# A cosine-attention and GELU kernel: the order of scores, roots and copies in the first batch

## The chip, the cores and the metric

The kernel runs on one core of a Trainium2 chip. The metric is the device time of one execution in microseconds (us). Before the change the median of five runs is 442.06 us (440.85 to 446.4).

## What is computed

For 8 batches, 12 heads, 448 positions and 64 dimensions, the rows of q and k are divided by their norms, scores are divided by tau = 0.1, and softmax and the product with v follow. The heads of a batch are then laid side by side as 3584 rows of 768, which go through two dense layers with an exact GELU between them:

```python
q_n = q / (np.linalg.norm(q, axis=-1, keepdims=True) + 1e-06)
k_n = k / (np.linalg.norm(k, axis=-1, keepdims=True) + 1e-06)
scores = np.matmul(q_n, k_n.transpose(0, 1, 3, 2)) / tau
attn = softmax(scores)            # over the last axis
x = np.matmul(attn, v) -> 3584 x 768
h = x @ w_in                      # 768 x 2048
out = (0.5 * h * (1 + erf(h / sqrt(2)))) @ w_out   # 2048 x 768
```

## The kernel before

The six **pairs** of heads of a batch are numbered g (0 to 5 for the first batch). The 448 positions are four **chunks** of 112. For each pair:

- `load_qk` (L101) brings q and k on SyncE's queue, `load_v` (L115) brings v on GpSimd's queue (its second call serves pairs 1 and 2).
- `square` (L125) and `reduce` (L139) make the sums of squares. Squares of pairs 1 and 2 run on ScalarE, that of pair 3 on VectorE, later ones on GpSimd. All reductions run on VectorE.
- `root` (L151) takes the roots: two small ScalarE operations (`lq`, `root`), then two small VectorE ones (`se`, `rn`).
- `scale` (L170) multiplies q and k by `rn` and writes them as bf16 (`qkb`). GpSimd does it, but for the q half of pair 0, which VectorE does.
- `transposes` (L181) turns `qkb` on TensorE into a PSUM tile `tp`, and VectorE copies it to `qkT`. Pair 0 has two half tiles (`tp0`, `tp0b`) and two half copies (L194); the other pairs of the first batch have one copy (L197). Later batches use a DMA transpose.
- `scores` (L200) multiplies a chunk of k with all of q into the PSUM tile `st`, of which there are two, and ScalarE takes the exponential into `pt` (L209), 192 times in the kernel.
- `columns` (L219) multiplies `pt` of two pairs with ones (`sm`, the sums) or v (`o`). `reciprocals` (L233) and `normalise` (L242) are VectorE's work behind them; `normalise` writes `x`, the input of the dense layers.

The tiles `tp`, `spin`, the second `o` of a pair and later `hp` and `op` share two PSUM banks that `mm_tile` (L89) hands out in turn; `aside=1` asks for the other one without taking a turn.

The order on every engine is the order in which the code is written: scheduling is manual, and each engine runs its list in order, waiting where an operand isn't there. `upto(f, n)` calls f for the next items until n are done. `spin(n)` issues n TensorE matmuls on constants whose result nobody reads. The work before the loop (L461 on) loads, and takes pairs 0 and 1 as far as the scaling. `attention_first` (L327) is the first batch: its loop runs over g, and one turn of it is called a **slot** here. A slot holds the scores of pair g, and beside them the preparation of the pairs behind it and the columns of the pairs ahead of it. Behind the loop the columns of pairs 4 and 5 are done chunk by chunk, and then `first(0)` runs the first dense layer of the batch (`hp`, L432, with the GELU at L454). From the second batch on `attention` interleaves the scores with pieces of the second dense layer (`op`, L268). These parts aren't touched.

Of the kernel before, what the change touches and what calls it, by code (L numbers as in the profile page):

```python
# [15 lines left out]
def kernel(  # L16
# [21 lines left out]
    HP = H // 2  # L38
# [50 lines left out]
    def mm_tile(name, shape=(128, 512), dtype=F32, aside=None):  # L89
        t = ps_mm.tile(list(shape), dtype, tag=f"mm{turn[0] if aside is None else turn[0] ^ aside}", name=name)  # L90
        if aside is None:
            turn[0] ^= 1
        return t
# [19 lines left out]
    NV = len(v_parts)  # L113
# [86 lines left out]
    def scores(g, c0, n=2):  # L200
        qkT = qkT_t[g]
        for c in range(c0, c0 + n):
            st = ps_st.tile([128, 2, 512], F32, tag="st", name=f"st{g}_{c}")
            for h in range(2):
                rows = slice(h * D, (h + 1) * D)
                nc.tensor.matmul(st[:CS, h, :S], lhsT=qkT[rows, 1, c, :], rhs=qkT[rows, 0, :, :],  # L206
                                 start=True, stop=True)
            pt = ptp.tile([CS, 2, S], BF16, tag="pt", name=f"pt{g}_{c}")
            nc.scalar.activation(pt, st[:CS, :, :S], AF.Exp, scale=inv_tau)  # L209
            pt_t[g, c] = pt  # L210
# [8 lines left out]
    def columns(g, n, chunks=range(NC), aside=0):  # L219
        if chunks[0] == 0:  # L220
            bank_t[g, n] = (mm_tile(f"o{g + 1}", aside=aside) if n == 2 else
                            ps_acc.tile([128, 512], F32, tag=("sm", "o")[n], name=("sm", "o")[n] + str(g)))
        for c in chunks:
            for j in range(2):
                for h in range(2):
                    r = 32 * (2 * j + h)
                    w = v_t[g + j][:, h, c, n - 1:D:2] if n else ones
                    nc.tensor.matmul(bank_t[g, n][r:r + 32, :S], lhsT=w, rhs=pt_t[g + j, c][:, h, :],  # L228
                                     start=(c == 0), stop=(c == NC - 1), tile_position=(0, r))
# [3 lines left out]
    def reciprocals(g):  # L233
        tr = rcp.tile([128, S // 32, 32], F32, tag="tr", name=f"tr{g}")
        nc.vector.transpose(tr.rearrange("p b r -> p (b r)"), bank_t.pop((g, 0))[:, :S])  # L235
        rc = rcp.tile([128, S // 32], F32, tag="rc", name=f"rc{g}")
        nc.vector.reciprocal(rc, tr[:, :, 0])
        rs = rcp.tile([128, S // 32, 32], F32, tag="rs", name=f"rs{g}")
        nc.vector.transpose(rs, rc.to_broadcast([128, S // 32, 32]))  # L239
        rs_t[g] = rs.rearrange("p b r -> p (b r)")  # L240

    def normalise(g):  # L242
        b, p = divmod(g, HP)
        rs = rs_t.pop(g)
        for n in (2, 1):
            nc.vector.tensor_tensor(x_t[b][:, p + n - 1, :], bank_t.pop((g, n))[:, :S], rs, ALU.mult)  # L246
# [62 lines left out]
    def upto(f, n, last=NG):  # L309
        while done.get(f, 0) < min(n, last):  # L310
            done[f] = done.get(f, 0) + 1
            f(done[f] - 1)

    def roots(n):
        upto(root, n, len(groups))


    def spin(n):
        if n == 0:
            return  # L320
        ps = mm_tile("spin")
        for _ in range(n):
            nc.tensor.matmul(ps[:CS, :S], lhsT=ident, rhs=blank, start=True, stop=True)  # L323
# [3 lines left out]
    def attention_first():  # L327
        x_t[0] = xp.tile([128, HP, S], BF16, tag="x", name="x0")
        for g in range(HP):
            scores(g, 0)  # L330
            if g == 0:
                upto(square, 4)
                upto(reduce, 4)
                roots(3)
                upto(scale, 3)
                scores(g, 2, 1)
            if g < HP - 1:
                upto(transposes, g + 2)
            upto(reduce, min(g + 4, HP))
            if g == 3:  # L340
                columns(0, 1)
            elif g == 5:
                columns(2, 2, aside=1)
                normalise(2)
            else:
                spin((0, 4, 1, 0, 0)[g])
            if g == 4:
                columns(2, 0)
                reciprocals(2)
            scores(g, *((2, 2) if g else (3, 1)))  # L350
            if g == 2:
                columns(0, 0)
                reciprocals(0)
            if g == 3:
                columns(0, 2, aside=1)
                normalise(0)
            if g == 4:
                columns(2, 1)
            roots(min(g + 4, HP))
            upto(square, (5, 6, 6, 7, 8, 9)[g])  # L360
            upto(scale, min(g + 4, HP))
            upto(reduce, (0, 0, 0, 6, 7, 8)[g])
            upto(load_v, (2, 3, 3, 3, 3, 4)[g], NV)
            upto(load_wi, (1, 2, 3, 4, 4, 4)[g])
            upto(load_qk, (6, 6, 7, 8, 9, 12)[g])
            if g < HP - 2:
                spin((4, 5, 1, 2)[g])
        upto(load_wo, 2)
        upto(reduce, HP + 3)

        for c in range(NC):
            for n in range(3):
                columns(HP - 2, n, (c,))
        reciprocals(HP - 2)
        normalise(HP - 2)

# [95 lines left out]
    upto(square, 3)  # L472
    upto(scale, 1)
    upto(reduce, 2)
    roots(2)
    upto(scale, 2)
    upto(load_v, 2, NV)
    upto(load_wi, 1)
    upto(transposes, 1)
    spin(5)  # L480
    upto(reduce, 3)

    fill = []
    for b in range(B):
        if b == 0:
            attention_first()
        else:
            attention(b, fill)
        first(b)
        sb, hf = divmod(b, 2)  # L490
        todo = [(t, ni) for t in (range(3) if hf == 0 else range(3, 7)) for ni in range(2)]
        if b == 0:
            todo.sort(key=lambda x: x[1])
        fill = [f for t, ni in todo for f in second_pieces(sb, t, ni)]
# [37 lines left out]
```

## Time and profile before

| | |
|---|---|
| median of five runs | 442.06 us |
| the profiled execution, its own time | 442.58 us |
| its span in the trace | 440.5 us |
| first exponential of the first batch starts at | 13.71 us |
| last exponential of the first batch ends at | 38.09 us |
| first dense layer (`hp`) starts at | 39.45 us |
| TensorE busy | 97% of the span |
| ScalarE busy | 60% |
| VectorE busy | 37% |
| GpSimd busy | 46% |

The part that the change rewrites lies between about 9 and 39.45 us of a span of 440.5 us. Times below are microseconds from the start of the span. A busy share says little about one stage; the timeline of a stage, which gives the start, the duration, the line and the tiles of each instruction and what ended the idle time ahead of it, says which engine is waited for. PEclk is the clock that TensorE was granted, as a share of full speed.

### The profile page before, as it was taken

To read this page: it belongs to the slowest core of one execution; us is meant where nothing else is said; L and a number is where in the kernel's file an instruction comes from. 1 tells how busy PE (TensorE), PEld (TensorE's weight loads), DVE (VectorE), ACT (ScalarE), POOL (GpSimd) and SP (SyncE) were. 2 spreads that over 40 slices of the span, in tenths; PEclk is the share of its full clock that TensorE was granted. 3 is DMA by queue.
4 is the path that set the end of the run, shared out by engine and by line. 5 is a ranking of instruction groups with operands and counts; after the bars stand their busy time and mean duration, and the time that the engine had idled before them with its cause. 6 is when DMAs were issued, how large, how long until landed. Compare 5 with 4: busy or idle time off the path is not lost.

```text
span 440.5 us, 7927 instructions
## 1 busy us (share of the span) xinstructions
PE 428.6 (97%) x3294; PEld 216.0 (49%) x3294; DVE 164.8 (37%) x266; ACT 264.0 (60%) x380; POOL 203.3 (46%) x185
## 2 busy tenths in 40 slices
PE   7899999999999999999999999999999999999996
PEld 4444544555444544455444544445444554445563
DVE  4767214650255404542154501753045330341021
ACT  4696577736766467754767449655766458773300
POOL 2799936580834609291571906655190732300000
PEclk9699999999999999999999999999999999999999
DMA  8989999892683918756186743849077500711022
GB/s 228 245 188 209 190 190 214 215 209 63 101 163 83 214 24 112 172 108 159 24 150 146 147 120 45 173 123 207 4 129 152 128 8 1 131 37 36 1 71 71
DMA packets 83635, 54.97 MB, mean 125 GB/s; under 512 B 41872, under 2 KB 78608, under 8 KB 83600
## 3 DMA queue, kind: packets, MB, share of 16 engines
q1 hardware_dynamic: 66416, 42.35, 42.7%
q0 software_dynamic: 16784, 11.80, 18.9%
q8 instruction: 25, 0.41, 0.4%
q10 hardware_dynamic: 400, 0.33, 0.2%
q14 instruction: 10, 0.08, 0.1%
HBM read 45.61 MB, written 11.01 MB: 129 GB/s over the span
## 4 chain that ended last, share of the span: by engine, by line
PE 89%; ACT 5%; DMA 3%; DVE 1%; POOL 1%; SPq 0%; issue 0%; POOLq 0%; ACTq 0%
PE hp L432 33%; PE op L268 31%; PE st L206 10%; PE o L228 8%; PE sm L228 4%; ACT pt L209 4%; DMA qkT<-qkb 2%; DMA qk<-in_k_dram 2%; PE spin L323 1%; PE tp L192 1%; POOL qkb L176 0%; SPq L107 0%; ACT L456 0%; DVE x L246 0%; ACT sq L133 0%
## 5 line engine op out<-in xcount | busy, mean ns | idle before, releaser
L209 ACT ACTIVATE pt<-st 112x896 bf16<-112x896 f32 x192 | 164.7, 915 | 51.7 <-PE st L206 51.2
L268 PE MATMUL op<-wo,g 128*128 128x384 bf16 x896 | 157.9, 327 | 0.0
L432 PE MATMUL hp<-x,wi 128*128 128x448 bf16 x768 | 146.7, 353 | 0.0
L454 ACT ACTIVATE g<-hp 128x448 bf16<-128x448 f32 x128 | 67.1, 545 | 91.7 <-PE hp L432 91.4
L268 PEld LDWEIGHTS <-g 128*128 128x128 bf16 x896 | 81.9, 98 | 70.6 <-issue 21.6
L432 PEld LDWEIGHTS <-wi 128*128 128x128 bf16 x768 | 74.5, 98 | 71.6 <-issue 3.0
L176 POOL TENSOR_TENSOR qkb<-qk,rn 112x512 bf16<-112x512 f32 x95 | 96.8, 1044 | 13.6 <-DVE rn L167 12.2
L137 POOL TENSOR_TENSOR sq<-qk 112x1024 f32<-112x1024 f32 x44 | 82.3, 1888 | 4.4 <-DMA qk<-in_k_dram 4.4
L165 POOL TENSOR_SCALAR se<-sr 112x48 f32<-112x48 f32 x14 | 4.6, 326 | 152.7 <-ACT sr L164 152.6
L149 DVE TENSOR_REDUCE nq<-sq 112x16 f32<-112x1024 f32 x47 | 56.9, 1214 | 36.0 <-POOL sq L137 34.8
L206 PE MATMUL st<-qkT 64*112 64x448 bf16 x384 | 61.4, 380 | 3.4 <-ACT pt L209 3.3
L279 DVE COPY ot<-op 128x384 f32<-128x384 f32 x55 | 29.8, 541 | 78.5 <-PE op L268 78.5
L167 DVE RECIPROCAL rn<-se 112x48 f32<-112x48 f32 (+1 forms) x20 | 7.9, 393 | 103.8 <-POOL se L165 103.5
L228 PE MATMUL o<-pt,v 112*32 112x448 bf16 x768 | 41.4, 353 | 0.2 <-DVE x L246 0.2
L206 PEld LDWEIGHTS <-qkT 64*112 64x112 bf16 x384 | 21.2, 125 | 40.2 <-issue 37.5
L246 DVE TENSOR_TENSOR x<-o,rs 128x448 bf16<-128x448 f32 x48 | 27.8, 620 | 4.3 <-PE o L228 2.0
L235 DVE STREAM_TRANSPOSE tr<-sm 128x448 f32<-128x448 f32 x24 | 15.6, 650 | 35.8 <-PE sm L228 35.8
L228 PEld LDWEIGHTS <-v 112*32 112x32 bf16 x768 | 20.3, 97 | 16.1 <-issue 1.1
L228 PE MATMUL sm<-pt,ones 112*32 112x448 bf16 x384 | 23.1, 355 | 0.0
L323 PE MATMUL spin<-blank,ident 112*112 112x448 bf16 x46 | 13.6, 445 | 4.1 <-DVE qkT L194 2.8
L239 DVE STREAM_TRANSPOSE rs<-rc 128x448 f32<-128x448 f32 x24 | 15.5, 645 | 0.8
L120 POOL DMA_DIRECT2D v<-in_v_dram x17 | 14.0, 823 | 0.0
(37 smaller groups left out, 81.0 us busy)
## 6 DMA issues: line engine op xcount, KB each, us to landing
qk<-in_q_dram SPq DMA_DIRECT2D x48, 224.0 KB, 5.7
qk<-in_k_dram SPq DMA_DIRECT2D x47, 224.0 KB, 6.0
v<-in_v_dram POOLq DMA_DIRECT2D x15, 336.0 KB, 6.2
wi<-in_moe_w_in_dram POOLq DMA_DIRECT2D x4, 768.0 KB, 10.2
wo<-in_moe_w_out_dram POOLq DMA_DIRECT2D x4, 768.0 KB, 19.1
out_dram<-ot SPq DMA_DIRECT2D x7, 336.0 KB, 3.6
out_dram<-ot SPq DMA_DIRECT2D x8, 288.0 KB, 2.6
out_dram<-ot SPq DMA_DIRECT2D x8, 240.0 KB, 3.5
```

Of the source, the lines that this page charges most:

```text
L137: nc.gpsimd.tensor_tensor(sq, t, t, ALU.mult)
L149: nc.vector.tensor_reduce(nq, sq, mybir.AxisListType.X, ALU.add)
L176: eng.tensor_tensor(qkb[:, i].rearrange("p c h d -> p h c d"), t[:, i], rn[:, i].to_broadcast([CS, 2, NC, D]), ALU.mult)
L206: nc.tensor.matmul(st[:CS, h, :S], lhsT=qkT[rows, 1, c, :], rhs=qkT[rows, 0, :, :], start=True, stop=True)
L209: nc.scalar.activation(pt, st[:CS, :, :S], AF.Exp, scale=inv_tau)
L228: nc.tensor.matmul(bank_t[g, n][r:r + 32, :S], lhsT=w, rhs=pt_t[g + j, c][:, h, :], start=(c == 0), stop=(c == NC - 1), tile_position=(0, r))
L246: nc.vector.tensor_tensor(x_t[b][:, p + n - 1, :], bank_t.pop((g, n))[:, :S], rs, ALU.mult)
L268: nc.tensor.matmul(ps[:, :NH], lhsT=g_t[sb][:, kf, t * 128:(t + 1) * 128], rhs=wo[:, kf, ni * NH:(ni + 1) * NH], start=(kf == 0), stop=(kf ...
L279: nc.vector.tensor_copy(ot[:, lo:hi], ps[:, :NH])
L323: nc.tensor.matmul(ps[:CS, :S], lhsT=ident, rhs=blank, start=True, stop=True)
L432: nc.tensor.matmul(hps[m], lhsT=wi[:, kd, m * 128:(m + 1) * 128], rhs=x_t[b][:, kd, :], start=(kd == order[0]), stop=(kd == order[-1]))
L454: nc.scalar.activation(g_t[sb][:, m, hf * S:(hf + 1) * S], hps.pop(m), AF.Gelu)
```

## The change

It alters only the order of the first batch, the number of `spin` matmuls and the bank of one tile.

- Ahead of the loop, the transposes of pair 0 with their two half copies come ahead of `se` and `rn` of pair 1, and two spins follow in place of five. The second load of v leaves this place.
- In slot 0 the chunk-2 scores come ahead of the transposes of pair 1 as before, but the fourth reduction comes behind the copy of pair 1, the roots of pair 2 are the only ones, and the second load of v is issued behind the scaling of pair 2, which is behind the first load of `wi`.
- In slots 1 to 5 the roots of pair g + 2 (in place of g + 3) stand between the first two exponentials and the last two. The transposes of pair g + 1 come behind all four score chunks of pair g. `normalise(0)` comes ahead of the transposes of pair 4.
- Spins per slot were (4), (4, 5), (1, 1), (2) and are (4), (4, 3, 2), (4) and none from slot 3 on.
- Loads of v and `wi` in slots 1 and 2 come ahead of the scaling of pair 4 and of pair 5.
- The second `o` of pairs 2 and 4 swap banks.

```diff
             if g == 0:
                 upto(square, 4)
-                upto(reduce, 4)
                 roots(3)
                 upto(scale, 3)
-                scores(g, 2, 1)
-            if g < HP - 1:
-                upto(transposes, g + 2)
-            upto(reduce, min(g + 4, HP))
-            if g == 3:
-                columns(0, 1)
-            elif g == 5:
-                columns(2, 2, aside=1)
-                normalise(2)
+                upto(load_v, 2, NV)
+                scores(0, 2, 1)
+                upto(transposes, 2)
+                upto(reduce, 4)
+                scores(0, 3, 1)
+                spin(4)
             else:
-                spin((0, 4, 1, 0, 0)[g])
-            if g == 4:
-                columns(2, 0)
-                reciprocals(2)
-            scores(g, *((2, 2) if g else (3, 1)))
-            if g == 2:
-                columns(0, 0)
-                reciprocals(0)
-            if g == 3:
-                columns(0, 2, aside=1)
-                normalise(0)
-            if g == 4:
-                columns(2, 1)
-            roots(min(g + 4, HP))
+                roots(min(g + 3, HP))
+                upto(scale, min(g + 3, HP))
+                if g < 3:
+                    spin(4)
+                elif g == 3:
+                    columns(0, 1)
+                elif g == 4:
+                    columns(2, 0)
+                    reciprocals(2)
+                else:
+                    columns(2, 2)
+                    normalise(2)
+                scores(g, 2)
+                if g == 1:
+                    spin(3)
+                elif g == 3:
+                    columns(0, 2, aside=1)
+                    normalise(0)
+                upto(transposes, min(g + 2, HP))
+                upto(reduce, min(g + 4, HP))
+                if g == 1:
+                    spin(2)
+                elif g == 2:
+                    columns(0, 0)
+                    reciprocals(0)
+                elif g == 4:
+                    columns(2, 1)
             upto(square, (5, 6, 6, 7, 8, 9)[g])
-            upto(scale, min(g + 4, HP))
             upto(reduce, (0, 0, 0, 6, 7, 8)[g])
             upto(load_v, (2, 3, 3, 3, 3, 4)[g], NV)
             upto(load_wi, (1, 2, 3, 4, 4, 4)[g])
             upto(load_qk, (6, 6, 7, 8, 9, 12)[g])
-            if g < HP - 2:
-                spin((4, 5, 1, 2)[g])
...
-                columns(HP - 2, n, (c,))
+                columns(HP - 2, n, (c,), aside=1)
...
     upto(reduce, 2)
+    upto(transposes, 1)
+    spin(2)
     roots(2)
     upto(scale, 2)
-    upto(load_v, 2, NV)
     upto(load_wi, 1)
-    upto(transposes, 1)
-    spin(5)
     upto(reduce, 3)
```

## The prediction

> **What bounds it now.** The page first: TensorE is busy through the span and carries the chain that ended last, and its clock is low in one slice, the second.
>
> ```profile
> PE   7899999999999999999999999999999999999996
>
> PE 89%; ACT 5%; DMA 3%; DVE 1%; POOL 1%; SPq 0%; issue 0%; POOLq 0%; ACTq 0%
> ```
>
> So a stage that starts later on TensorE is not made good behind it, and I take any shift of the first dense layer (`hp`, 39.45) one to one into the end. Second, the stretches of 3.41 us between the clock's steps (us of the stretch, its length, then busy us of TensorE, its weight loads, VectorE, ScalarE, GpSimd, the granted clock, DMA share, GB/s):
>
> ```profile
> 6.49:9.90 3.41, 2.68 (x19) 1.76 (x18) 1.89 (x4) 1.40 (x4) 1.54 (x1) 1.00 1.11 272
> 9.90:13.32 3.42, 1.20 (x7) 0.68 (x8) 2.40 (x6) 1.38 (x3) 1.42 (x2) 1.00 1.18 264
> 13.32:16.73 3.41, 2.77 (x17) 1.34 (x16) 3.34 (x6) 2.94 (x5) 2.10 (x3) 0.50 1.12 258
> 16.73:20.14 3.41, 3.41 (x17) 1.77 (x18) 0.84 (x3) 2.50 (x5) 3.39 (x3) 0.50 1.21 233
> 23.56:26.97 3.41, 2.84 (x34) 1.42 (x32) 2.65 (x5) 3.38 (x6) 3.41 (x4) 1.00 0.59 161
> ```
>
> After a stretch with 1.20 us of 3.42 busy (35%) the clock was 0.50 for 6.82 us; 79% (2.68) and 83% (2.84) kept it, 81% (2.77) at half clock did not bring it back, a full stretch did. Third, the timeline, VectorE and the exponentials:
>
> ```profile
> 9.14 1.22 DVE L149 TENSOR_REDUCE nq<-sq 112x16 f32<-112x1024 f32 x1 [1.13 <-ACT sq L133]
> 11.35 0.19 DVE L160 TENSOR_REDUCE se<-root 112x16 f32<-112x32 f32 x1 [0.99 <-ACT root L159]
> 11.74 0.33 DVE L194 COPY qkT<-tp 128x448 bf16<-128x448 bf16 x1
> 11.98 0.37 DVE L194 COPY qkT<-tp0b 128x448 bf16<-128x448 bf16 x1
> ...
> 30.23 1.16 DVE L246 TENSOR_TENSOR x<-o,rs 128x448 bf16<-128x448 f32 x2 [1.30 <-PE o L228]
> 31.74 0.62 DVE L197 COPY qkT<-tp 128x896 bf16<-128x896 bf16 x1 [0.36 <-PE tp L192]
> ```
>
> ```profile
> 13.71 1.73 ACT L209 ACTIVATE pt<-st 112x896 bf16<-112x896 f32 x2 [2.39 <-PE st L206]
> 18.97 1.73 ACT L209 ACTIVATE pt<-st 112x896 bf16<-112x896 f32 x2 [0.86 <-PE st L206]
> 27.13 1.73 ACT L209 ACTIVATE pt<-st 112x896 bf16<-112x896 f32 x2
> 31.06 1.73 ACT L209 ACTIVATE pt<-st 112x896 bf16<-112x896 f32 x2 [0.32 <-PE st L206]
> ```
>
> The half copies sit 0.99 us behind a root. From 13.71 to the last exponential (38.09), 24 exponentials of 0.87 (half of 1.73) and four roots of 0.5 make 22.9 of 24.4 us: the stage is nearly ScalarE's, and only 2.05 us ahead of it plus 1.5 us of gaps inside are to be had.
>
> **Prices, all from this timeline.** TensorE, full / half clock: the scores of a chunk 0.32 (25.17 to 25.49) / 0.55 (16.09 to 16.64), of two chunks 0.52 / 0.92; from scores' start to exponential 0.44 (30.62 to 31.06) / 0.66 (18.31 to 18.97); transposes 0.50 / 0.86; four spins 0.88 (five took 1.09) / 1.67; `sm` or `o` 0.87. A score tile is free 0.96 behind its exponential's start (13.71 to 14.67). `lq` starts 1.61 behind the first of two exponentials (13.71 to 15.32), the next exponential 0.50 later. GpSimd: scaling 2.04, square 1.88, a DMA issue 0.8.
>
> **Step 1, half copies first.** VectorE is free at 10.33. The copies start there and end at 10.94; the spins follow 0.38 behind the first (as 11.74 to 12.12), at 10.71; two take 0.51, scores at 11.22, exponential at 11.66, **2.05 earlier**. `se` still waits for its root (11.35), so `qkb` of pair 1 still ends at 13.94: that cover makes the move free on VectorE.
>
> **Step 2, slot 0.** Roots of pair 2 move with the exponentials: 13.27 to 13.82. VectorE reduces at 11.74, squares pair 3 from 12.87 to 14.49, then `se`, `rn` at 14.50 and 14.72; the fourth reduction, now behind the copy, is out of the way. Scaling of pair 2 goes from 16.75 to 15.05, done at 17.1. But TensorE: idle to 10.71, busy to 11.85, chunk 2 at 12.62 (11.66 + 0.96), idle to 14.0 (`qkb`). In 9.90 to 13.32 that is some 1.55 us busy, 45%, of which 1.4 comes from rows of step 1. The trace shows a drop at 35% and none at 79%; 45% is nearer to the drop. I take **half clock from 13.32 to 20.14**, as before.
>
> The Trainium skill, "TensorE: Matmul & The Clock Gate", Part 1 on the clock gate, states that the clock is halved after at least one idle window of about 3.4 us. The longest idle here was 2.78 us and the clock did drop; by the rule the changed kernel, with gaps of at most 1.4 us, would stay at full clock, which gives the sum of rival 1; by the row it gives mine.
>
> At half clock: transposes 14.0, chunk 3 at 14.86, its exponential 15.52, spins 15.41 to 17.08, scores of pair 1 at 17.08, exponential **17.74** (18.97): 1.23 left.
>
> **Step 3, slots 1 and 2.** Four spins 18.0 to 19.67, chunk 2 at 19.67, exponential 20.3 (roots ended at 19.9), chunk 3 20.2 to 20.5, three spins 0.7, transposes to 21.7 (now behind all scores), copy 0.62 from 21.8, so pair 2 at 22.45, exponential **22.9** (23.41): 0.5 left; the spins ate the rest. Slot 2 is at full clock: chunk 2 at 23.86, chunk 3 at 24.73, transposes 25.05, `sm` 25.55, pair 3 at 26.42, exponential **26.86** (27.13): 0.27 left. GpSimd is no bound here: 17.1, load of v 17.9, square 19.8, scaling of pair 3 20.5 to 22.6, square 24.4, loads of v and `wi` now ahead 26.1, scaling of pair 4 to 28.1, 1.6 late by its own list and still ahead of its use at 29.87. SyncE's loads that wait for these scalings move by at most 1.7 us and serve the second batch. Nothing waits for them here.
>
> **Step 4, slot 3: a new wait.** `o` of pair 0 at 27.15, chunks 2 and 3 at 28.02 and 28.68, second `o` 29.0 to 29.87, transposes of pair 4 to 30.37. On VectorE `x` stands ahead of the copy now (row 30.23: `x` waits for `o`). It starts at 29.97; two take 1.07 to the next start, copy 31.04 to 31.66, pair 4 at 31.7, exponential **32.14**, where before it was 31.06. Last exponential of slot 3 ends at 30.7: ScalarE idles 1.4 us. That is a **loss of 1.1**. In slot 4 the copy stands behind the three operations of `reciprocals` and `o` ahead of the scores: `sm` 32.22, transposes of pair 5 34.29 to 34.79, `o` to 35.66, exponential of pair 5 at **36.1** (34.68): 1.42 late.
>
> **Step 5, end.** Slot 5: `o` to 37.05, chunk 3 at 37.93, so the columns of pairs 4 and 5 run from 38.25, four times 0.57 (37.25 to 37.81) to 40.53. The bank swap may save the 0.21 us that `o` waited for `x` at 37.25. `hp` at 40.55 against 39.45: **+1.1**. 442.58 + 1.1 = 443.7 for the profiled execution; that stood 0.52 above the median, so 443.2 on the median. The clock's price: at half clock the thirteen spins of slots 0 and 1 cost twice; without the drop see rival 1.
>
> **An operation that no row shows:** the second v behind `wi` on GpSimd's queue. Before, v was issued at 13.88 and landed in 6.9, `wi` at 14.65 in 10.5, so both at 25.1. v is now issued at 17.1: between 17.1 + 6.9 = 24.0 and 17.1 + 10.5 = 27.6; needed at 27.15. I take 25.1, the time both had landed: nothing, at most 0.45.
>
> **Rival 1, full clock stays (faster).** For: 45% may be above a limit that lies between 35% and 79%. Then spins take 0.88, exponentials of pairs 1, 2, 3 start at 16.15, 20.69, 24.64; the scaling of pair 4 ends at 27.4, just in time for 27.65; the wait of step 4 is there too: pair 4 at 29.99, pair 5 at 33.95, `hp` at 38.6: -0.85, **441.2**.
>
> **Rival 2, the clock drops a second time (slower).** Place: 30.38 to 33.80, where step 4 leaves TensorE idle 1.33 us (30.37 to 31.7) and little else: some 60% busy. If the limit lies above 60%, half clock from 33.80 for 6.82 us costs up to 3.4 us of TensorE's work on top: **446.6**. Against: 79% kept it, and 60% is nearer to that. It decides from a limit of 60% on.
>
> **Rival 3, the change doesn't bring the early start**: v lands late and `o` of pair 0 holds TensorE in slot 3. +0.45 on my forecast, 443.7; on rival 1 27.6 - 24.95 = 2.65, giving 443.9.
>
> **Numbers.** Forecast 0.58, rival 1 0.27, rival 2 0.11, rival 3 0.04. The range, 440.2 to 445.2, takes in rival 1 less the 1.2 us by which the fastest run lies under the median, and the forecast with v late and half of rival 2's price; what is left out is rival 2 at full price and the tails. A measurement of this kernel tells about 1% (4.4 us) from no change: slower beyond that 0.06 (half of rival 2), faster 0.01, within 0.93.
>
> **What would show it.** First exponential at about 11.7; a half clock somewhere from 13 to 20; pair 1 near 17.7; in slot 3 `x` ahead of the copy and some 1.4 us of ScalarE idle; `hp` at 40.5. Wrong if the clock stays (`hp` before 39), if `o` waits for v, or if a later stage gives the shift back.

## The result and the profile after

The changed kernel took **442.81 us** (median of 42 executions) against 441.80 us of the kernel before (77): ratio 1.0018, 95% interval 1.0009 to 1.0027. By the ratio that is 0.8 us slower, a fifth of one per cent (the two medians lie 1.0 us apart). The forecast was 1.1 us slower.

The profiled execution of the changed kernel was one of its quickest, 441.42 us with a span of 439.6, and the loads of q and k came early in it. ScalarE's square of pair 1 waits for its load in the profile before and starts at 8.05 us; in the profile after it follows the operation ahead of it without a wait, at 6.53 (ScalarE's timelines, before and then after):

```profile
8.05 1.06 ACT L133 ACTIVATE sq<-qk 112x1024 f32<-112x1024 f32 x1 [1.27 <-DMA qk<-in_k_dram]
```

```profile
6.53 1.06 ACT L133 ACTIVATE sq<-qk 112x1024 f32<-112x1024 f32 x1
```

The two profiles are laid on each other at that instruction. (At the square of pair 2, 9.81 and 8.21, the shift would be 1.60 us in place of 1.52, so the column "moved" is good to about 0.1 us.) Counted from the start of the square of pair 1:

| start, counted from the square of pair 1 | before | after | moved | forecast |
|---|---|---|---|---|
| first exponential (13.71; 10.10) | 5.66 | 3.57 | -2.09 | -2.05 |
| pair 1 (18.97; 16.74) | 10.92 | 10.21 | -0.71 | -1.23 |
| pair 2 (23.41; 21.24) | 15.36 | 14.71 | -0.65 | -0.5 |
| pair 3 (27.13; 25.16) | 19.08 | 18.63 | -0.45 | -0.27 |
| pair 4 (31.06; 30.43) | 23.01 | 23.90 | +0.89 | +1.08 |
| pair 5 (34.68; 34.34) | 26.63 | 27.81 | +1.18 | +1.42 |
| first dense layer (39.45; 38.83) | 31.40 | 32.30 | +0.90 | +1.1 |

(Each row from pair 1 on is the first exponential of that pair. Pair 3 after is its scores' start, 24.72, and the 0.44 from there to an exponential.)

The page after shows none of this: TensorE still carries the chain, and the clock is still low in the second slice and nowhere else.

```profile
PEclk9699999999999999999999999999999999999999
PE 91%; ACT 5%; DVE 1%; POOL 1%; DMA 1%; issue 1%; POOLq 0%
```

The clock steps down at 11.24 us and up again at 18.07, two stretches of 3.41 us later. Stretches of that length counted from these steps say more (the columns are those of the prediction's second view):

```profile
7.83:11.24 3.41, 1.86 (x16) 0.95 (x14) 3.07 (x7) 2.62 (x5) 1.68 (x2) 1.00 1.15 259
11.24:14.66 3.42, 2.08 (x13) 1.05 (x12) 2.22 (x6) 1.93 (x5) 3.40 (x4) 0.50 1.14 274
14.66:18.07 3.41, 3.41 (x11) 1.39 (x11) 1.06 (x1) 2.11 (x3) 3.40 (x4) 0.50 1.13 250
28.31:31.72 3.41, 2.12 (x30) 0.91 (x28) 1.85 (x4) 1.91 (x3) 3.41 (x3) 1.00 1.11 214
```

The clock halves after a stretch in which TensorE was busy for 1.86 of 3.41 us (55%), and stays so for 6.83 us. The last line is slot 3, where the new wait leaves TensorE busy for 2.12 us (62%); there the clock held.

ScalarE's timeline has the pairs' exponentials, and the gap of 1.50 us ahead of pair 4:

```profile
10.10 1.73 ACT L209 ACTIVATE pt<-st 112x896 bf16<-112x896 f32 x2 [0.38 <-PE st L206]
16.74 1.73 ACT L209 ACTIVATE pt<-st 112x896 bf16<-112x896 f32 x2 [1.30 <-PE st L206]
21.24 1.73 ACT L209 ACTIVATE pt<-st 112x896 bf16<-112x896 f32 x2 [0.68 <-PE st L206]
27.23 1.71 ACT L209 ACTIVATE pt<-st 112x896 bf16<-112x896 f32 x2
30.43 3.34 ACT L209 ACTIVATE pt<-st 112x896 bf16<-112x896 f32 x4 [1.50 <-PE st L206]
34.34 3.34 ACT L209 ACTIVATE pt<-st 112x896 bf16<-112x896 f32 x4 [0.57 <-PE st L206]
```

VectorE's and TensorE's show why: `x` first, the copy of pair 4 behind it, and TensorE, behind the transposes, idle until that copy is done. TensorE's first line is the scores of pair 3, its last the first dense layer.

```profile
28.25 1.16 DVE L246 TENSOR_TENSOR x<-o,rs 128x448 bf16<-128x448 f32 x2 [0.42 <-PE o L228]
29.32 0.61 DVE L197 COPY qkT<-tp 128x896 bf16<-128x896 bf16 x1
```

```profile
24.72 0.76 PE L206 MATMUL st<-qkT 64*112 64x448 bf16 x4
28.13 0.57 PE L192 MATMUL tp<-ident,qkb 112*128 112x112 bf16 x8
29.99 0.59 PE L206 MATMUL st<-qkT 64*112 64x448 bf16 x4 [1.29 <-DVE qkT L197]
38.83 3.39 PE L438 MATMUL hp<-x,wi 128*128 128x448 bf16 x17
```

### The profile page after: what moved, and what is told of

It reads as the page before. It is cut to its first block, busy times and chain, and to the rows that moved or that the text cites. A ratio compares the mean times of both kernels' runs of the same rounds, so it can differ in the third digit from the quotient of the medians.

```text
span 439.6 us, 7921 instructions
## 1 busy us (share of the span) xinstructions
PE 426.7 (97%) x3291; PEld 214.4 (49%) x3291; DVE 164.5 (37%) x266; ACT 263.9 (60%) x380; POOL 204.3 (46%) x185
## 4 chain that ended last, share of the span: by engine, by line
PE 91%; ACT 5%; DVE 1%; POOL 1%; DMA 1%; issue 1%; POOLq 0%
PE hp L438 33%; PE op L268 33%; PE st L206 11%; PE o L228 8%; PE sm L228 5%; ACT pt L209 4%; POOL qkb L176 1%; PE spin L323 1%; DMA qk<-in_q_dram 1%; PE tp L192 0%; DVE nq L147 0%; DVE qkT L197 0%; DVE x L246 0%; DVE sq L131 0%; DVE ot L276 0%
## 5 line engine op out<-in xcount | busy, mean ns | idle before, releaser
L176 POOL TENSOR_TENSOR qkb<-qk,rn 112x512 bf16<-112x512 f32 x95 | 97.8, 1055 | 11.8 <-DVE rn L167 11.6
L323 PE MATMUL spin<-blank,ident 112*112 112x448 bf16 x43 | 12.3, 436 | 1.5 <-POOL ident masks.py:199 1.3
```

Of the source, the lines that this page charges most:

```text
L176: eng.tensor_tensor(qkb[:, i].rearrange("p c h d -> p h c d"), t[:, i], rn[:, i].to_broadcast([CS, 2, NC, D]), ALU.mult)
```

## The experiments

All ratios are to the kernel before, run beside the experiment, with 95% intervals. The theory was the forecast's: an early start of 2 us, most of which the half clock takes, and a new wait in slot 3 that costs more than is left.

### e1: the slot-3 order put back

```diff
                 elif g == 3:
-                    columns(0, 2, aside=1)
+                    upto(transposes, 5)
+                    columns(0, 2)
                     normalise(0)
```

> The changed kernel with one thing put back: in slot 3 the transposes of pair 4 and their copy come ahead of the second o of pair 0 and of normalise(0). Theory A (the new wait in slot 3 is what costs): the exponential of pair 4 starts 1.3 us earlier, ScalarE's idle time ahead of it falls from 1.4 to some 0.1 us, and the first dense layer starts 0.9 to 1.1 us earlier than in the changed kernel: ratio to the kernel before about 0.9995 (0.998 to 1.000), where the changed kernel has 1.0018. Theory B (the clock and the spins take the early start, slot 3 only hides it): the time gained in slot 3 is lost again in slots 4 and 5 and the ratio stays at 1.0015 or more.

Measured: 441.51 us, ratio **0.9992** (0.9978 to 1.0007). The changed kernel has 1.0018, so the slot-3 order alone is worth about 0.0026, 1.1 us; that is theory A's number. In its profile the exponentials run from slot 3 into slot 4 without a gap, and the dense layer starts 30.76 us behind the square of pair 1 (37.55 and 6.79), where it was 32.30 in the changed kernel. (Of these 1.54 us, 0.18 stand already at pair 2, 21.32 in e1: the clock was low there for one stretch only, 13.68 to 17.09.) The two views are ScalarE's and TensorE's timeline of this experiment:

```profile
27.31 5.18 ACT L209 ACTIVATE pt<-st 112x896 bf16<-112x896 f32 x6
```

```profile
37.55 2.63 PE L439 MATMUL hp<-x,wi 128*128 128x448 bf16 x13
```

This edit moves the copy and the second `o` together, so it prices the order of slot 3 as a whole.

### e2: the half copies alone

```diff
     upto(reduce, 2)
+    upto(transposes, 1)
+    spin(2)
     roots(2)
     upto(scale, 2)
     upto(load_v, 2, NV)
     upto(load_wi, 1)
-    upto(transposes, 1)
-    spin(5)
```

(in the kernel before)

> The kernel before with step 1 alone: the transposes and half copies of pair 0 ahead of se and rn of pair 1, and two spins for five. Theory A (the early start is real, but only part of it gets through the half-clock stretch): first exponential 2 us earlier, pair 1 about 1.2 earlier, later slots 0.3 to 0.5, ratio 0.999. Theory B (the early start is lost wholly to the clock, since three spins fewer leave TensorE less busy): ratio 1.000 or above, with a half clock at least as long as before.

Measured: 441.57 us, ratio 0.9996 (0.9982 to 1.0011): the time can't tell the two apart. The profile can, in part. Behind the square of pair 1 (6.99) the first exponential comes 3.72 us later, 1.94 earlier than before. Pair 1 at 17.50 is 0.41 earlier, and pair 2 at 22.29 is 0.06 earlier. The early start is real and is gone by pair 2, which is nearer to theory B. Its half clock lasts 6.83 us (12.54 to 19.37), and GpSimd's scaling of pair 1 takes 3.02 us there in place of 2.04, which neither theory had; e9 comes back to that.

### e3: TensorE's gaps filled

```diff
     upto(transposes, 1)
-    spin(2)
+    spin(7, st=True)
     roots(2)
...
                 upto(load_v, 2, NV)
+                spin(4)
                 scores(0, 2, 1)
+                spin(5)
                 upto(transposes, 2)
                 upto(reduce, 4)
                 scores(0, 3, 1)
-                spin(4)
```

With `st=True` the spins write into a tile of `ps_st`, which is free then, and so don't wait for a half copy.

> The changed kernel with its idle TensorE time from the transposes of pair 0 to those of pair 1 filled: seven spins into a score tile that do not wait for the half copy in place of two that do, four behind the first two score chunks and five ahead of the transposes of pair 1, and none of the four that stood behind chunk 3. Theory A (the half clock takes the early start): no stretch falls to half clock between 9 and 21 us, the mean granted clock rises from 0.991 to 0.996 or more in most runs, pair 1 starts 1.5 us earlier, the dense layer 1.5 to 2 us earlier than in the changed kernel: ratio to the kernel before 0.997 to 0.999. Theory B (the clock costs little because these slots wait for ScalarE and GpSimd anyway): ratio stays within 0.0005 of 1.0018.

Measured: 444.83 us, ratio **1.0068** (1.0042 to 1.0094), 3 us slower and neither theory's number. In the profile the first part of theory A held: from 9 to 21 us the granted clock is 1.00, and pair 2's exponential at 19.60 is 12.80 behind the square of pair 1 (6.80), 1.9 earlier than in the changed kernel. Then TensorE stands still in slot 3 (TensorE's timeline, then two stretches of this experiment):

```profile
23.75 0.37 PE L228 MATMUL o<-pt,v 112*32 112x448 bf16 x2
25.57 1.28 PE L228 MATMUL o<-pt,v 112*32 112x448 bf16 x14 [1.45 <-DMA v<-in_v_dram]
```

```profile
22.61:26.02 3.41, 1.96 (x30) 0.77 (x24) 3.17 (x7) 2.90 (x5) 3.40 (x5) 1.00 1.16 227
26.02:29.44 3.42, 3.42 (x32) 0.88 (x25) 0.17 (x1) 1.73 (x2) 3.40 (x5) 0.50 1.22 206
```

`o` of pair 0 waits 1.45 us for the second load of v, which the change put behind `wi` in GpSimd's queue, and after that stretch (57% busy) the clock halves for another 3.42 us, in the slot that is already late. These are the prediction's rivals 3 and 2, together, as soon as the slots ahead are fast. The profile doesn't explain the whole 3 us: this execution took 442.66 us at a mean granted clock of 0.994, and eight of the twelve had 0.991 or less, with a median of 445.76 us, so they lost more of the clock at places that no profile shows. The one execution that kept the clock, at 1.000, took 441.16 us.

### e4: filled gaps and slot-3 order

The edits of e1 and e3 together.

> The two edits together, the slot-3 order of the kernel before and the filled gaps. Theory A: the gains add, 1.0 and 1.5 to 2 us under the changed kernel: ratio 0.995 to 0.997. Theory B (one bound behind both, as the scaling of pair 4 on GpSimd, now behind two DMA issues): not faster than the better of the two alone by more than 0.3 us.

Measured: 442.50 us, ratio 1.0014 (0.9993 to 1.0034). Not the sum of theory A, and slower than e1 alone. `o` waits for v here too, without a drop of the clock in this execution (TensorE's timeline of e4):

```profile
26.23 0.94 PE L228 MATMUL o<-pt,v 112*32 112x448 bf16 x14 [1.51 <-DMA v<-in_v_dram]
```

Theory B's wording holds, but its candidate (GpSimd's scaling of pair 4) isn't what the profile names; the load of v is.

### e5: v ahead of wi

```diff
                 roots(3)
                 upto(scale, 3)
-                upto(load_v, 2, NV)
+                upto(load_wi, 1)
...
     upto(scale, 2)
-    upto(load_wi, 1)
+    upto(load_v, 2, NV)
     upto(reduce, 3)
```

> The changed kernel with the second load of v and the first load of wi changing places on GpSimd's list, so v is ahead of wi in the queue as before the change; nothing else. Theory A (v behind wi is a cost of the e3 kind only where the slots ahead are fast; in the changed kernel o of pair 0 comes at 25.4 or later and v has just landed): within 0.5 us of the changed kernel, ratio 1.001 to 1.002. Theory B (v is late in the usual execution of the changed kernel, and its profile was a lucky one): 1 us or more faster, ratio 0.999 to 1.000.

Measured: 442.62 us, ratio 1.0020 (0.9998 to 1.0042), the same as the changed kernel and as theory A had it. In the changed kernel itself v's place costs nothing that can be measured.

### e6, e7, e8: v ahead of wi, with the other edits

e6 is e3 with the exchange of e5, e7 is e4 with it (all three edits), e8 is e1 with it.

> The kernel with filled gaps (e3) and v ahead of wi. Theory A (e3 was slow because o of pair 0 waited 1.45 us for v and the clock then dropped in slot 3): no wait for v, no half clock, ratio 0.997 to 0.999, some 3.5 us under e3. Theory B (e3 was slow for its spins): stays above 1.004.

> Filled gaps, the slot-3 order of the kernel before, v ahead of wi. Theory A (three separate costs): pair 3 from 24, pair 4 from 28, first dense layer near 36.8 to 37.3, ratio 0.994 to 0.996. Theory B (the loads of q and k, or GpSimd's scaling of pair 4 at 25 to 27, bound slot 3 next): ratio 0.997 to 0.999.

> The changed kernel with the slot-3 order of the kernel before and v ahead of wi, gaps not filled. Theory A: as the slot-3 order alone, 0.999, since at half clock v is in time. Theory B (v late in many executions): 0.997 to 0.998.

Measured: e6 441.59 us, ratio 0.9993 (0.9970 to 1.0016); e7 **439.99 us, ratio 0.9954** (0.9928 to 0.9981); e8 440.82 us, ratio 0.9977 (0.9955 to 0.9999). In e6's profile `o` of pair 0 starts at 24.52 without a wait and the clock doesn't drop, so v's place was what stopped e3. For e6 and e7 theory A came near (e6 a little above its 0.997 to 0.999); e8 has theory B's number, but no profile shows v late in it. Together with the runs above that is each edit measured with and without the others:

| edit | from, to | change of the ratio |
|---|---|---|
| slot-3 order | after to e1; e3 to e4; e5 to e8; e6 to e7 | -0.0026; -0.0054; -0.0043; -0.0039 |
| gaps filled, v late | after to e3; e1 to e4 | +0.0050; +0.0022 |
| gaps filled, v early | e5 to e6; e8 to e7 | -0.0027; -0.0023 |
| v early, gaps not filled | after to e5; e1 to e8 | +0.0002; -0.0015 |
| v early, gaps filled | e3 to e6; e4 to e7 | -0.0075; -0.0060 |

Each ratio carries an interval of about 0.001 to 0.0027 to each side, and e1 to e4 ran on another chip than e5 to e8, so only the sign and the size of the larger steps are to be read. The slot-3 order gains 1.1 to 2.4 us wherever it is put back. Filling the gaps gains 1.0 to 1.2 us if v is in time (the smaller of the two, e8 to e7, is not clear of noise), and loses 1 to 2.2 us if it isn't. In e7 ten of twelve executions had a mean granted clock of 0.998 or more, with a median of 439.83 us; with the gaps filled it was one in e3, four in e4, nine in e6 and eight in e10. Where the half copies come early and the gaps aren't filled, it was none in the changed kernel, e1, e2, e5 and e8, and two in e9.

e7 beats both kernels, and its profile shows a place where gain is lost again. The dense layer starts 29.75 us behind the square of pair 1 (6.91), 1.65 earlier than in the kernel before, but in the second batch TensorE then waits 1.39 us (TensorE's timeline of e7):

```profile
36.66 3.58 PE L440 MATMUL hp<-x,wi 128*128 128x448 bf16 x18
71.37 0.59 PE L206 MATMUL st<-qkT 64*112 64x448 bf16 x4 [1.39 <-DMA qkT<-qkb]
```

The scores wait for a transpose by DMA. e2 (1.41 us) and e6 (1.74 us) have the wait at the same place in their profiles, e1, e4 and e9 a shorter one (0.46, 0.49 and 0.23), and the profiles before and after have none. In the profile before the same scores start at 72.92, so counted from the square of pair 1 those of e7 are 0.41 us ahead (64.46 against 64.87). This execution of e7 took 440.74 us, 0.75 over the kernel's median; how many executions meet the wait isn't known.

### e9 and e10: VectorE's square away from GpSimd's scaling

The profile after has one thing that the forecast did not: GpSimd's second half of the scaling of pair 1 takes 2.02 us in place of 1.03, just while VectorE squares pair 3. GpSimd's timelines before (both halves) and after (the second half), and VectorE's after:

```profile
11.90 2.04 POOL L176 TENSOR_TENSOR qkb<-qk,rn 112x512 bf16<-112x512 f32 x2 [2.99 <-DVE rn L167]
```

```profile
11.30 2.02 POOL L176 TENSOR_TENSOR qkb<-qk,rn 112x512 bf16<-112x512 f32 x1
```

```profile
11.21 1.21 DVE L135 TENSOR_TENSOR sq<-qk 112x1024 f32<-112x1024 f32 x1
```

e9 is the changed kernel, e10 is e7, both with:

```diff
             if g == 0:
-                upto(square, 4)
                 roots(3)
...
                 upto(transposes, 2)
+                upto(square, 4)
                 upto(reduce, 4)
```

> The changed kernel with VectorE's square of pair 3 behind the copy of pair 1, where before it stood behind the reduction of pair 2 and ran beside GpSimd's scaling of pair 1. Theory A (the two engines get in each other's way: the second half of that scaling took 2.02 us beside the square, in place of 1.03): the scaling of pair 1 takes 2.0 us in place of 3.0, its transposes start 1 us earlier, and pair 1's first exponential 0.7 to 1 us earlier; the ratio to the kernel before 0.999 to 1.001, where the changed kernel has 1.0018. Theory B (the second half is slow for another reason, such as loads that land): it still takes 2 us, and nothing moves.

> The same move of the square in the kernel with all three edits (filled gaps, slot-3 order, v ahead of wi). Theory A: pair 1 and all later slots up to 0.5 to 1 us earlier, the first dense layer too; ratio 0.9935 to 0.9955, if the second batch does not take it back in its wait for transposes by DMA. Theory B: as that kernel, 0.9954, or worse since the scaling of pair 2 now meets the square.

Measured: e9 443.42 us, ratio 1.0024 (0.9993 to 1.0056); e10 441.12 us, ratio 0.9971 (0.9951 to 0.9990). Both miss the numbers of theory A. The mechanism of theory A is there, and the gain is not. In e9 the scaling of pair 1 is back at 2.04 us, and the scaling of pair 2, which now meets the square, takes 3.03 (GpSimd, then VectorE, then TensorE of e9):

```profile
10.51 2.04 POOL L176 TENSOR_TENSOR qkb<-qk,rn 112x512 bf16<-112x512 f32 x2 [1.41 <-DVE rn L167]
...
13.35 3.03 POOL L176 TENSOR_TENSOR qkb<-qk,rn 112x512 bf16<-112x512 f32 x2
```

```profile
13.66 1.83 DVE L135 TENSOR_TENSOR sq<-qk 112x1024 f32<-112x1024 f32 x1
```

```profile
24.28 0.94 PE L228 MATMUL o<-pt,v 112*32 112x448 bf16 x14 [0.77 <-DMA v<-in_v_dram]
```

So the delay follows the overlap from one scaling to the other. Pair 1's exponential comes 7.70 us behind the square of pair 1 (14.57 and 6.87), 2.5 earlier than in the changed kernel, more than the move alone explains: in this execution the clock did not fall (1.00 from 9 to 19 us). And with the slots ahead fast, `o` waits 0.77 us for v again. e9's twelve executions spread from 439.13 to 445.62 us; two had a mean clock of 0.998 or more and took 439.13 and 440.22. In e10 slot 3 is bound by GpSimd: the transposes of pair 4 wait 0.43 and 0.63 us for the halves of its scaling, TensorE is busy for 2.12 of 3.42 us (62%), and the clock halves at 27.08. Since the clock differs so much between executions, e9 leaves open what the collision costs in the changed kernel at an equal clock.

## Why the prediction was right, point by point

**Step 1** held: the first exponential moved by 2.09 us, forecast 2.05. **Step 2** held in its main point, the half clock, and missed one term. "`qkb` of pair 1 still ends at 13.94: that cover makes the move free on VectorE" was wrong. The copies themselves are free, but the reduction and the square behind them move up too, and the square now runs beside the scaling. That scaling took 3.02 us in place of 2.04 and ended 0.90 us later, counted from the square of pair 1 (13.32 - 6.53 against 13.94 - 8.05). TensorE made some of it good by transposing the first half while it waited for the second, and pair 1 gained 0.71 us where 1.23 was forecast (TensorE's timeline after):

```profile
11.48 0.55 PE L192 MATMUL tp<-ident,qkb 112*128 112x112 bf16 x4
13.38 0.55 PE L192 MATMUL tp<-ident,qkb 112*128 112x112 bf16 x4 [1.34 <-POOL qkb L176]
```

The profile before had signs of it: GpSimd's half of the scaling of pair 0 took 1.54 us while VectorE scaled the other half, and the square took 1.62 us where it began beside the end of the scaling of pair 1 (VectorE's timeline before):

```profile
13.40 1.62 DVE L135 TENSOR_TENSOR sq<-qk 112x1024 f32<-112x1024 f32 x1
```

The step's own times put the square from 12.87 to 14.49 beside a scaling that ended at 13.94, without a price for it. The Trainium skill, "SBUF — State Buffer", sections "Who interferes with whom" and "SBUF: two separate sides", has the rule: a VectorE operation with two SBUF inputs and a GpSimd operation that reads SBUF take a shared port pair in turn, and the one that comes second is blocked for the whole of the first. The trace agrees: the square began first, at 11.21, and the half that met it took 0.99 us more, against 1.21 us of square.

**Step 3** came out close, 0.65 and 0.45 us left at pairs 2 and 3 against 0.5 and 0.27, and the first of the two numbers is luck. From pair 1's exponential to pair 2's the forecast had 5.16 us (17.74 to 22.9), and it took 4.50 (16.74 to 21.24). The clock was back at 18.07, 1.33 us behind pair 1's exponential, where the forecast had it back 2.40 us behind (20.14), so the spins and scores of slot 1 cost less than was worked out. This error of 0.66 us made good the 0.52 us that step 2 had missed.

**Step 4** held and is shown. The gap ahead of pair 4 is 1.50 us (forecast 1.4), the swing from pair 3 to pair 4 is 1.34 us (0.45 gained to 0.89 lost; forecast 0.27 and 1.08), and e1, which puts that order back, gains 1.1 us. **Step 5**: the dense layer moved by +0.90 in the laid-on profiles and the program by 0.8, forecast 1.1. The 0.2 us between forecast and profile stand already at pair 3 (0.45 against 0.27); slots 3 to 5 behind it went as worked out, to 0.06 us.

Two sums of the prediction are slightly off and decide nothing. The gaps that ScalarE's rows show between 13.71 and 38.09 add up to 2.14 us and not 1.5 (0.86, 0.64, 0.16, 0.32 and 0.16), and the range by its own terms is 440.0 to 445.4.

**The clock.** "Half clock from 13.32 to 20.14, as before" took the one profile before for every execution. It isn't so. Of 93 executions of the kernel before that ran beside the experiments, 31 had a mean granted clock of 0.998 or more (median 441.08 us), and 51 one of 0.990 to 0.994 (442.07), as in its profile. Of 42 executions of the changed kernel none had 0.998 or more, and 31 had 0.990 to 0.994, with 442.81 us. Between the two groups of 0.990 to 0.994 the change costs 0.74 us; that is rough, since the 51 come from three chips with medians of 441.58, 442.07 and 443.15 us. A third of the executions of the kernel before has no drop, and the changed kernel has lost that: this is a second cost, which the prediction didn't have. It doesn't stand in for the wait in slot 3: e1, none of whose twelve executions had 0.998 or more, is at 0.9992.

The prediction weighed a rule of the Trainium skill, "TensorE: Matmul & The Clock Gate", Part 1: half rate after at least one idle window of about 3.4 us. Read as 3.4 us without work, it fails a second time here: the clock of the changed kernel fell after a stretch that was 55% busy, with no idle time in it longer than 0.82 us.

**The rivals.** Rival 1 (the clock stays) did not come in any of the 42 executions. Rival 2 put 60% busy on slot 3, and the profile has 62% there, with the clock held. But five of the 42 executions had a mean clock of 0.984 to 0.988 (median 443.98 us), where in the profiles one stretch at half clock shows as 0.994 to 0.996 and two as 0.990 to 0.992. So in about one of eight the clock was probably low for a third stretch or more; whether in slot 3 isn't shown, since none of them was profiled. Rivals 2 and 3 did not decide the median; e3 shows both of them once the front is fast. What rival 1 left out is this wait. The prediction did put a late v on rival 1, as rival 3 and at 443.9 us, but as an unlikely case, though its own numbers had v needed at 24.95 and landing at 25.1; and it did not see that the wait could bring the second drop of the clock with it. e3 with both is at 444.8 us; its one execution at full clock, 441.16, is at rival 1's 441.2.

## What to carry to other kernels

A step that is put early in a stage is worth what is left of it at the stage's end, so follow it to the last slot and look for the place where the new order makes one engine do long work ahead of a short copy that another engine waits for: here 2.1 us at the front were 0.45 us three pairs later, and one copy that stood behind a normalisation made 0.9 us of loss of them. When instructions move up on VectorE, list what GpSimd does at the new time, since two-input work on the one stretched the other's by nearly its own length (0.99 us by a square of 1.21). And where several costs lie in a row, undo them together as well as singly: filling the gaps lost 2 us alone and gained 1 us once the load ahead of it was in time.

## What the runs showed of the hardware that was not expected

- A GpSimd `tensor_tensor` of 1.03 us took 2.02 us beside a VectorE `tensor_tensor` of 1.21 us (changed kernel); in e9, where the square met another scaling, that pair took 3.03 us in place of 2.04 and the square 1.83 us.
- Counted from the clock's steps, in stretches of 3.41 us, the clock fell behind stretches in which TensorE was 35% busy (before, e1), 38% (e5), 41% (e8), 55% (after), 57% (e3), 62% (e10) and 64% (e2), and held behind others with 59% (e2, 70.57 to 73.98), 62% (after; e5, 26.96 to 30.37) and 63% (e3, 29.43 to 32.84). So in these profiles it is lost somewhere about 60%, and between 59% and 64% the busy share doesn't say which way. e2 has both in one execution; behind the first of these stretches the clock fell, behind the second it held:

```profile
9.13:12.54 3.41, 2.19 (x16) 1.06 (x16) 2.96 (x7) 3.13 (x6) 1.58 (x3) 1.00 1.13 230
70.57:73.98 3.41, 2.00 (x14) 0.88 (x12) 2.19 (x3) 1.41 (x3) 0.26 (x1) 1.00 1.51 136
```

- A drop lasted one stretch (3.41 us) where TensorE was then busy through (99% or 100%: e1, e3, e5, e8, e10), and two where the first at half clock was 53% (e2), 61% (after) or 82% busy (before) and the second 100%.
- The load of k for pair 1 lands at least 1.7 us apart between profiles (ScalarE's square of pair 1 starts at 6.36 without a wait for it in e8 and waits for it until 8.05 in the kernel before), and the second batch's wait for a transpose by DMA is 1.39 to 1.74 us in the profiles of e2, e6 and e7, 0.23 to 0.49 in e1, e4 and e9, and absent from those before and after. Two profiles of a change of 1 us can't be compared without taking these out.
